# The output projection in two accumulators by halves, 48 weight chunks kept in SBUF, two more kept in PSUM, transposes 32 columns wide

## The chip, the cores and the metric

The kernel runs on one core of a Trainium2 chip. TensorE (PE) multiplies matrices, VectorE (DVE), ScalarE (ACT) and GpSimd (POOL) do the rest, and SyncE (SP) issues most of the DMAs. The metric is the device time of one execution in microseconds; lower is better.

## What is computed

The output is two independent results side by side, each 2048 x 1024 in bf16. A is a long convolution done with FFTs; the change does not touch it. B is a transformer layer over 64 segments of 32 rows, in which 8 memory rows go from one segment to the next:

```python
mem = mem0                                              # 8 x 1024
for s in range(64):
    h = concatenate([mem, x[32*s : 32*s + 32]])         # 40 x 1024
    q, k, v = h @ Wq, h @ Wk, h @ Wv                    # 32 heads of 128: 40 x 4096 each
    p = softmax(where(mask, q @ k.T * 128**-0.5, -1e9)) # per head, 40 x 40
    o = concat_heads(p @ v) @ Wo                        # 40 x 4096 @ 4096 x 1024
    mem, out[s] = o[:8], o[8:]
```

A segment cannot start before the first 8 rows of the one before are done, so the 64 segments run one after the other, and each uses all four weight matrices: 32 MB in bf16, more than SBUF holds.

## The kernel before

**Prologue.** A's stages run first, for some 350 us. Beside and behind them, B's projections of the rows that need no memory are prepared: 24 of the 32 rows go through the segment loop, and the keys, queries and values of the other 8 are computed for all segments at once and stored in DRAM (`REC`, `VBD`). The last of it is the dense value product (`vb_ps`, L765), whose results leave through staging tiles `pair` in the buffers `wring2` and `wring3` by a store into `VBD` on ACT's queue (L768). A planner orders the prologue; the segment loop stands in a block whose order is the program's (`manual_schedule`), so each engine and queue there works in the order of the text, waiting where data or buffers are not ready.

**Chunks.** The weights are cut into 64 chunks of 128 x 2048 (512 KB): 8 for each half (g) of K, Q and V, and 16 for the output (one for two heads). `order` lists them as a segment uses them. 47 are resident in SBUF (`Wmid`, `Wres`, `Wmore`, `Wlate`, `pw`). The other 17, at the places `STREAM` of the order, are copied once to the DRAM buffer `WS` and come from there in each segment through a ring of six slots (`wring`, `RING`): when a chunk's last use is done, `done` gives its slot back and calls `fetch`, which issues the next load in the order on SP's queue (L724). The sixth slot (`wring2`) joins in segment 0 after the chunk at `LATE_SLOT`.

**Kept chunks.** PSUM has columns that the segments do not use. Chunk "A" (an output chunk) is copied there in segment 0 (`keep`), and from segment 1 on it does not come from DRAM: four copies (`quarter`, L817) bring it back to SBUF by quarters, through the buffers `rot` and `QT`, between output chunks. Of chunk "B" five eighths lie in PSUM: the load of the ring brings 768 of its 2048 columns (L721) and `move` (L800) copies the rest from PSUM into the ring slot.

**A segment.** `hT`, the rows of h transposed, comes as the tile `rec` (`load_x`, a POOL DMA, issued when the values' second half is done); the 8 memory columns are put in by `fill_mem`: two transposes of Y on TensorE into `tps` (L862) and a DVE copy into `rec` (L863), in two halves (output columns 0 to 255 and 256 to 511 of both column halves). K half 0 needs chunks 0, 1, 4, 5 from the first fill and 2, 3, 6, 7 from the second, hence `K0_ORDER`. `Proj.run` (L918) takes four products a chunk, each 32 columns of the array wide and 512 columns long, on four column tiles that work side by side. ACT copies an accumulator to `qkv_sb` (L927); four full transposes (L933) and a copy make keys `KT` and queries `QT`. Then scores (L939, L942) into `SB`, softmax on DVE and ACT, attention into `OTp` (L980, L984), ACT's copy to `OT` (L992), and the output: `project` (L1002) takes four products a chunk, 64 columns wide and 512 long, on two column tiles, all into one accumulator `yacc` of one PSUM bank. At the end ACT copies `yacc` to `Y` in two halves (L1078), and the next segment starts with `fill_mem`.

The accumulators `acc` and `yacc` take turns in two PSUM banks (`ps_acc`). Tiles of the pool `one` have one buffer a tag, so a new tile under a tag waits for the last reader of the one before. Two engines' accesses to one PSUM bank of a tile are put in order by waits.

## Time and profile before

| | |
|---|---|
| median of 3 runs | 1903.21 us (1902.97 to 1905.81) |
| the profiled execution | 1907.36 us, span 1905.6 us |
| granted TensorE clock, mean | 0.982 |
| busy: PE, DVE, ACT, POOL | 92%, 45%, 35%, 18% of the span |
| segment 0 starts; its output is stored | 445.8 us; 476.3 us |
| loads of wring: whole; 192 KB | 961; 63 |

PE's busy time is that of matmuls, whose ends are modelled; weight loads run beside them. "Idle before" is the time that an engine stood still ahead of an instruction, with what ended it. A chain of waits is followed back from the last instruction to what released each one. The DMA share is the mean busy share of the core's 16 DMA engines.

### The profile page before, as it was taken

The page shows a single profiled execution, that of the slowest core. Times are in us where ns is not written, and L with a number is a line of the kernel's source. Part 1 is how long each engine was busy: PE and PEld are TensorE (multiplying, and loading weights), DVE is VectorE, ACT ScalarE, POOL GpSimd, SP SyncE. Part 2 cuts the span into 40 slices and gives each one's busy share as a digit, 9 for nine tenths or more (in the row PEclk, how much of TensorE's full clock was granted, in tenths as well). Part 3 has the DMA queues.
Part 4 walks back from the last instruction along what each step waited for, and adds up shares of the span by engine and source line. Part 5 has one row for each costly group of instructions (what it writes and reads, how often), then busy time and mean ns, then how long its engine had stood idle before and what let it go on. Part 6 is the DMA issues. An engine that isn't in the chain of part 4 may idle for free.

```text
span 1905.6 us, 62245 instructions
## 1 busy us (share of the span) xinstructions
PE 1749.0 (92%) x26353; PEld 831.1 (44%) x26353; DVE 853.8 (45%) x2812; ACT 674.8 (35%) x1195; POOL 342.8 (18%) x1014
## 2 busy tenths in 40 slices
PE   6989986778999999999999999999999999999998
PEld 3433322333444444444444444444444444444444
DVE  9927863202344444444444444444443444444443
ACT  6945640112333333333333333333333333333333
POOL 4003341000121111111121111111111111111111
PEclk9999998989999999999999999999999999999999
DMA  9989889998999999999999999999999999999998
GB/s 338 351 302 329 291 271 333 327 284 277 349 373 374 373 378 373 377 372 373 373 373 378 373 376 372 370 372 372 379 374 369 371 378 374 375 373 371 372 379 311
DMA packets 251211, 678.00 MB, mean 356 GB/s; under 512 B 74850, under 2 KB 82930, under 8 KB 250932
## 3 DMA queue, kind: packets, MB, share of 16 engines
q1 hardware_dynamic: 178692, 604.26, 85.0%
q0 software_dynamic: 17488, 46.70, 7.0%
q10 hardware_dynamic: 54752, 23.07, 4.5%
q8 instruction: 206, 3.38, 0.7%
q14 instruction: 73, 0.60, 0.1%
HBM read 618.35 MB, written 59.24 MB: 356 GB/s over the span
## 4 chain that ended last, share of the span: by engine, by line
PE 80%; DMA 7%; DVE 5%; issue 4%; ACT 2%; POOL 0%; ACTq 0%; SPq 0%; DVEq 0%; POOLq 0%
PE acc L918 38%; PE yacc L1002 22%; PE kb_ps L625 5%; PE tps L933 4%; DMA wring<-WS 3%; PE vb_ps L765 3%; DMA REC<-stage 2%; PE OTp L980 1%; ACT s_sb L243 1%; DVE rec L863 1%; PE SB L942 1%; PE tps L862 1%; PE s_ps L241 1%; DMA REC<-xt 1%; PE SB L939 1%
## 5 line engine op out<-in xcount | busy, mean ns | idle before, releaser
L918 PEld LDWEIGHTS <-rec 128*32 128x32 bf16 x12288 | 283.6, 96 | 300.2 <-DVE rec L863 60.7
L927 ACT CAST qkv_sb<-acc 128x512 bf16<-128x512 f32 x384 | 224.7, 585 | 480.0 <-PE acc L918 287.9
L1002 PEld LDWEIGHTS <-OT 128*64 128x64 bf16 x4348 | 255.1, 109 | 195.3 <-ACT OT L992 27.6
L918 PE MATMUL acc<-wring,rec 128*32 128x512 bf16 x2556 | 252.7, 382 | 22.8 <-DVE rec L863 19.1
L918 PE MATMUL acc<-Wres,rec 128*32 128x512 bf16 x3328 | 249.4, 380 | 0.6 <-issue 0.6
L1002 PE MATMUL yacc<-wring,OT 128*64 128x512 bf16 (+1 forms) x1540 | 235.9, 380 | 5.0 <-DMA wring<-WS 4.9
L918 PE MATMUL acc<-Wmid,rec 128*32 128x512 bf16 x3072 | 234.4, 382 | 0.0
L1002 PE MATMUL yacc<-Wmore,OT 128*64 128x512 bf16 (+1 forms) x1280 | 185.4, 381 | 0.0
L817 DVE TENSOR_SCALAR quarter<-OTp 128x256 int32<-128x256 int32 x252 | 101.1, 422 | 187.6 <-ACT OT L992 149.3
L1080 POOL DMA_DIRECT2D out_dram<-Y x128 | 63.7, 502 | 484.5 <-ACT Y L1078 484.2
L918 PE MATMUL acc<-pw,rec 128*32 128x512 bf16 x1796 | 144.8, 382 | 0.1
L1078 ACT CAST Y<-yacc 128x256 bf16<-128x256 f32 x128 | 41.4, 375 | 274.5 <-PE yacc L1002 274.5
L992 ACT CAST OT<-OTp 128x640 bf16<-128x640 f32 x128 | 88.6, 692 | 129.7 <-PE OTp L984 129.0
L918 PE MATMUL acc<-Wlate,rec 128*32 128x512 bf16 x1280 | 104.0, 384 | 17.1 <-DVE rec L863 17.1
L948 DVE TENSOR_REDUCE mx<-SB 128x5 f32<-128x200 f32 x128 | 47.1, 368 | 153.4 <-PE SB L942 153.3
L856 POOL DMA_DIRECT2D rec<-REC x64 | 36.2, 566 | 405.0 <-PE acc L918 372.1
L1002 PE MATMUL yacc<-Wlate,OT 128*64 128x512 bf16 x768 | 105.7, 383 | 0.2 <-ACT OT L992 0.2
L933 PEld LDWEIGHTS <-qkv_sb 128*128 128x128 bf16 x1024 | 57.8, 97 | 109.5 <-ACT qkv_sb L927 108.0
L933 PE MATMUL tps<-ident,qkv_sb 128*128 128x128 bf16 x1024 | 101.6, 222 | 0.4 <-ACT qkv_sb L927 0.3
L893 POOL COPY KT<-rec 128x128 bf16<-128x128 bf16 x128 | 38.2, 298 | 329.4 <-PE SB L942 324.2
L863 DVE COPY rec<-tps 128x32 bf16<-128x32 bf16 x128 | 22.3, 175 | 165.1 <-PE tps L862 115.8
L1027 DVE COPY KT<-tps 128x512 bf16<-128x512 bf16 x64 | 27.1, 424 | 152.2 <-PE tps L933 152.2
(215 smaller groups left out, 2392.9 us busy)
## 6 DMA issues: line engine op xcount, KB each, us to landing
wring<-WS SPq DMA_DIRECT2D x961, 512.0 KB, 6.0
rec<-REC POOLq DMA_DIRECT2D x64, 192.0 KB, 5.8
wring<-WS SPq DMA_DIRECT2D x63, 192.0 KB
SK<-s_sb SPq DMA_DIRECT2D x16, 512.0 KB, 4.8
SU<-s_sb SPq DMA_DIRECT2D x16, 512.0 KB, 4.9
Kg<-SK SPq DMA_DIRECT2D x32, 256.0 KB, 4.2
Ug<-SU SPq DMA_DIRECT2D x32, 256.0 KB, 5.7
REC<-stage ACTq DMA_DIRECT2D x16, 512.0 KB, 10.9
```

The costliest lines, as they stand in the source:

```text
L625: nc.tensor.matmul(ps[:], lhsT=ws[kc][:, hl * 128:(hl + 1) * 128], rhs=xbt(kc).rearrange("p s t -> p (s t)"), start=(kc == 0), stop=(kc == 7))
L765: nc.tensor.matmul(ps[:], lhsT=xbt(kc)[:, 16 * tb:16 * tb + 16, :].rearrange("p s t -> p (s t)"), rhs=ws[kc][:, c * 512:(c + 1) * 512], st ...
L817: nc.vector.tensor_scalar(out=t[:].bitcast(I32), in0=OTi[:, q, 160:416], scalar1=0, scalar2=None, op0=ALU.bitwise_or)
L863: nc.vector.tensor_copy(hT.rearrange("p (dh j) t -> p dh j t", dh=2)[:, :, 2 * half:2 * half + 2, 0:NM], tp.rearrange("p (j dh r) -> p dh ...
L918: nc.tensor.matmul(self.acc[32 * c:32 * c + 32, x - 512 * c:y - 512 * c], lhsT=hT[:, kc, :], rhs=r, start=(n_kc == 0 and x == 512 * c), st ...
L927: nc.scalar.copy(sb[:], self.acc[:])
L933: nc.tensor.transpose(tp[:, i * 128:(i + 1) * 128], sb[:, i * 128:(i + 1) * 128], ident[:])
L948: nc.vector.tensor_reduce(out=mx[:], in_=S, op=ALU.max, axis=AX.X)
L992: nc.scalar.copy(OT[:], o_view)
L1002: nc.tensor.matmul(yacc[64 * dh:64 * dh + m, x - o:y - o], lhsT=lhsT, rhs=r, start=(h == 0 and x == o), stop=(h >= 30), tile_position=(0, ...
L1078: nc.scalar.copy(Y[:, 256 * half:256 * half + 256], yacc[:, 256 * half:256 * half + 256])
L1080: nc.gpsimd.dma_start(bass.AP(outb.tensor, outb.offset + SEG * s * 2048 + 512 * dh, [[2048, 32], [1, 512]]), Y[64 * dh + NM:64 * dh + 40, :])
```

## The change

The output gets two accumulators in two PSUM banks, one for columns 0 to 255 of each half (f = 0), one for 256 to 511. An output chunk is now used in two `out_half` steps of four products, 256 columns long. The first four chunks (`FIRST`) do all of f = 0 before f = 1, and so do the last four (`LAST`). ACT copies the first half to Y between the two halves of `LAST`, and the first `fill_mem` of the next segment stands before the last half chunk. The second fill comes after three chunks of K instead of four.

Every transpose of 128 columns (`turn_tile`) is four products, each of 32 columns on its own column tile.

48 chunks are resident: the new one goes to the buffer `wring2`, which leaves five slots in the ring. 16 chunks are outside, and two of these, A and now all of B (the chunk kc = 4 of K's half 1), stay on chip after segment 0, so 14 are loaded in a segment. B lies in `tps`, `SB`, `OTp` and a small SBUF tile `B_rest`. `quarter_b` copies it by quarters into the buffers of `E` (the exponentials), `QT` and `rot`, and `Proj.add` takes the products in 16 of 128 columns (the last four each in two pieces). The copy of the transposed queries to `QT0` moves from DVE to ACT.

```diff
-STREAM = (0, 5, 10, 15, 21, 26, 31, 36, 41, 46, 49, 52, 54, 57, 60, 61, 63)
-KEPT = {14: "A", 4: "B"}
+STREAM = (1, 7, 13, 18, 20, 24, 30, 35, 41, 46, 49, 53, 56, 59, 60, 62)
+KEPT = {13: "A", 4: "B"}
+FIRST, LAST = (0, 1, 2, 3), (15, 11, 12, 14)
+O_ORDER = (*FIRST, 4, 5, 6, 7, 8, 9, 10, 13, *LAST)
 K0_ORDER = (0, 1, 4, 5, 2, 3, 6, 7)
...
 X_LOAD = 1
-RING = 6
-LATE_SLOT = 4
+RING = 5
...
         order += [(2, kc, g) for kc in range(8)]
-    for hp in range(16):
+    for hp in O_ORDER:
         order.append((3, hp, 0))
...
     loads = [(s, ch) for s in range(n_seg) for ch in order_s
-             if s == 0 and ch not in v_temp[2:] or s > 0 and kept.get(ch) != "A"]
+             if s == 0 and ch not in v_temp[2:] or s > 0 and ch not in kept]
     live = {}
...
             live[s, ch] = k, t = slot()
-            if s > 0 and ch in kept:
-                nc.sync.dma_start(t[:, 0:768], stream_src(ch)[:, 0:768])
-                move(kept[ch], t, True)
-            else:
-                nc.sync.dma_start(t[:], stream_src(ch))
+            nc.sync.dma_start(t[:], stream_src(ch))
...
                     place_late(4, stage_home)
+        place_late(1, lambda: base.tile([128, 2048], BF, tag="wring2", name="Wring"))
         assert len(late) == len(at_hand)
...
     OTi, tpi = OTp[:].bitcast(I32), tps[:].bitcast(I32)
-    homes = {"B": [(OTi[:, :, 416:512], slice(384, 768)), (tpi[:, 1, :], slice(768, 1024))]}
-
-    def move(name, t, back):
-        for p, cols in homes[name]:
-            w = t[:].bitcast(I32)[:, cols]
-            if len(p.shape) == 3:
-                w = w.rearrange("p (b x) -> p b x", b=4)
-            src, dst = (p, w) if back else (w, p)
-            nc.vector.tensor_scalar(out=dst, in0=src, scalar1=0, scalar2=None, op0=ALU.bitwise_or)
+    B_rest = one.tile([128, 4, 32], I32, name="B_rest")
+    B_homes = [tpi[:, 1, :].rearrange("p (c x) -> p c x", c=4),
+               SB[:].bitcast(I32)[:, 200:456].rearrange("p (c x) -> p c x", c=4),
+               OTi[:, :, 416:480], OTi[:, :, 480:512]]
+
+    def bits(dst, src):
+        nc.vector.tensor_scalar(out=dst, in0=src, scalar1=0, scalar2=None, op0=ALU.bitwise_or)
+
+    def quarter_b(q, tag):
+        n = 64 if q < 3 else 32
+        t = one.tile([128, 4, 2 * n], BF, tag=tag, name="quarter_b")
+        bits(t[:].bitcast(I32), B_homes[q])
+        w = [(512 * c + 128 * q, 512 * c + 128 * q + 2 * n, t[:, c, :]) for c in range(4)]
+        if q == 3:
+            w += [(512 * c + 448, 512 * c + 512, B_rest[:].bitcast(BF)[:, c, :]) for c in range(4)]
+        return w
...
             for q in range(4):
-                nc.vector.tensor_scalar(out=OTi[:, q, 160:416].rearrange("p (dh x) -> p dh x", dh=2),
-                                        in0=w[:, q // 2, q % 2], scalar1=0, scalar2=None, op0=ALU.bitwise_or)
+                bits(OTi[:, q, 160:416].rearrange("p (dh x) -> p dh x", dh=2), w[:, q // 2, q % 2])
         else:
-            move(kept[ch], t, False)
+            w = t[:].bitcast(I32).rearrange("p (c f x) -> p f c x", c=4, f=4)
+            for q in range(3):
+                bits(B_homes[q], w[:, q])
+            bits(B_homes[3], w[:, 3, :, 0:32])
+            bits(B_rest[:], w[:, 3, :, 32:64])
...
         t = one.tile([128, 512], BF, tag=("rot", "QT")[q % 2], name="quarter")
-        nc.vector.tensor_scalar(out=t[:].bitcast(I32), in0=OTi[:, q, 160:416], scalar1=0, scalar2=None,
-                                op0=ALU.bitwise_or)
+        bits(t[:].bitcast(I32), OTi[:, q, 160:416])
         return [(o, o + 256, t[:, 256 * dh:256 * dh + 256]) for dh, o in enumerate(quarter_cols(q))]
...
             place_late(1, at_hand[ch][1])
-        elif ch in streamed and (now[0] == 0 or kept.get(ch) != "A"):
+        elif ch in streamed and (now[0] == 0 or ch not in kept):
             if now[0] == 0 and ch in kept:
...
             free.append(live.pop((now[0], ch))[0])
-            i = order_s.index(ch)
-            if now[0] == 0 and i == LATE_SLOT:
-                free.append(2)
-                fetch()
             fetch()
...
+    def turn_tile(dst, src):
+        for e in range(0, 128, 32):
+            nc.tensor.matmul(dst[e:e + 32, :], lhsT=src[:, e:e + 32], rhs=ident[:], start=True, stop=True,
+                             is_transpose=True, tile_position=(0, e))
+
     def fill_mem(hT, Y, half):
...
         for j in (2 * half, 2 * half + 1):
-            nc.tensor.transpose(tp[:, j * 128:(j + 1) * 128], Y[:, j * 128:(j + 1) * 128], ident[:])
+            turn_tile(tp[:, j * 128:(j + 1) * 128], Y[:, j * 128:(j + 1) * 128])
         nc.vector.tensor_copy(
...
     with tc.manual_schedule():
-        for _ in range(RING - 3):
+        for _ in range(RING - 2):
             fetch()
...
+                def add(self, kc, w, start=False, stop=False):
+                    for c in range(4):
+                        for x, y, r in columns(w, 512 * c, 512 * c + 512):
+                            nc.tensor.matmul(self.acc[32 * c:32 * c + 32, x - 512 * c:y - 512 * c],
+                                             lhsT=hT[:, kc, :], rhs=r, start=start and x == 512 * c,
+                                             stop=stop, tile_position=(0, 32 * c))
+
                 def run(self, n=8):
...
                         ch = (self.m, kc, self.g)
-                        w = pieces(ch)
-                        for c in range(4):
-                            for x, y, r in columns(w, 512 * c, 512 * c + 512):
-                                nc.tensor.matmul(self.acc[32 * c:32 * c + 32, x - 512 * c:y - 512 * c],
-                                                 lhsT=hT[:, kc, :], rhs=r, start=(n_kc == 0 and x == 512 * c),
-                                                 stop=(n_kc == 7), tile_position=(0, 32 * c))
-                        done(ch)
+                        if s == 0 or ch not in kept:
+                            self.add(kc, pieces(ch), n_kc == 0, n_kc == 7)
+                            done(ch)
                     self.kc += n
...
                 for i in range(4):
-                    nc.tensor.transpose(tp[:, i * 128:(i + 1) * 128], sb[:, i * 128:(i + 1) * 128], ident[:])
+                    turn_tile(tp[:, i * 128:(i + 1) * 128], sb[:, i * 128:(i + 1) * 128])
                 return tp.rearrange("p (i c r) -> p i c r", i=4, c=4)
...
-            def project(h, w, OT):
+            def project(h, f, w, OT, stop=False):
                 k = 40 * (h % 16)
...
                 for dh in range(2):
-                    o = (h % 2) * 1024 + dh * 512
-                    for x, y, r in columns(w, o, o + 512):
-                        nc.tensor.matmul(yacc[64 * dh:64 * dh + m, x - o:y - o], lhsT=lhsT,
-                                         rhs=r, start=(h == 0 and x == o), stop=(h >= 30),
-                                         tile_position=(0, 64 * dh), skip_group_check=(h == 31))
+                    o = (h % 2) * 1024 + dh * 512 + f * 256
+                    for x, y, r in columns(w, o, o + 256):
+                        nc.tensor.matmul(yacc[f][64 * dh:64 * dh + m, x - o:y - o], lhsT=lhsT,
+                                         rhs=r, start=(h == 0 and x == o), stop=stop,
+                                         tile_position=(0, 64 * dh))
+
+            def out_half(hp, f, OT, stop=False):
+                w = pieces((3, hp, 0))
+                for hh in range(2):
+                    project(2 * hp + hh, f, w, OT, stop and hh == 1)
+                if f == 1:
+                    done((3, hp, 0))
...
                 for hp in hps:
-                    ch = (3, hp, 0)
-                    if s > 0 and kept.get(ch) == "A":
-                        continue
-                    w = pieces(ch)
-                    for hh in range(2):
-                        project(2 * hp + hh, w, OT)
-                    done(ch)
+                    for f in range(2):
+                        out_half(hp, f, OT)
...
                 hp = [ch[1] for ch in kept if kept[ch] == "A"][0]
-                project(2 * hp + q // 2, w, OT1)
-
-            fill_mem(hT, Y, 0)
-            k0 = Proj(0, 0).run(4)
+                project(2 * hp + q // 2, q % 2, w, OT1)
+
+            if s == 0:
+                fill_mem(hT, Y, 0)
+            k0 = Proj(0, 0).run(3)
             fill_mem(hT, Y, 1)
-            k0 = k0.run(4).evac()
+            k0 = k0.run(5).evac()
             q0 = Proj(1, 0).run(4)
...
             q0 = q0.run(4).evac()
-            k1 = Proj(0, 1).run(4)
+            k1 = Proj(0, 1)
+            if s > 0:
+                kb = [ch[1] for ch in kept if kept[ch] == "B"][0]
+                b0, b1 = quarter_b(0, "E"), quarter_b(1, "QT")
+                k1.run(1)
+                k1.add(kb, b0)
+                b2 = quarter_b(2, "E")
+                k1.run(2)
+                k1.add(kb, b1)
+            else:
+                k1.run(4)
             QT0 = one.tile([128, 4, 4, 32], BF, tag="QT", name="QT")
-            nc.vector.tensor_copy(QT0[:], transposes(q0))
-            k1 = k1.run(4).evac()
+            nc.scalar.copy(QT0[:], transposes(q0))
+            if s > 0:
+                b3 = quarter_b(3, "rot")
+                k1.run(3)
+                k1.add(kb, b2)
+                k1.add(kb, b3)
+            k1 = k1.run(8 - k1.kc).evac()
             scores(0, QT0, KT0)
...
             V1 = pv1.evac()
-            yacc = ps_acc.tile([128, 512], F32, tag="acc", name="yacc")
-            out_proj(range(0, 5), OT0)
+            yacc = [ps_acc.tile([128, 512], F32, tag="acc", name="yacc") for f in range(2)]
+            for f in range(2):
+                for hp in FIRST:
+                    out_half(hp, f, OT0)
+            out_proj((4,), OT0)
             attend(1, PT1, V1)
...
             if s == 0:
-                out_proj(range(5, 8), OT0)
-                out_proj(range(8, 16), OT1)
+                out_proj((5, 6, 7), OT0)
+                out_proj((8, 9, 10, 13), OT1)
             else:
                 w0 = quarter(0)
-                out_proj(range(5, 8), OT0)
+                out_proj((5, 6, 7), OT0)
                 w1 = quarter(1)
                 out_quarter(0, w0)
-                out_proj(range(8, 10), OT1)
+                out_proj((8,), OT1)
                 w2 = quarter(2)
                 out_quarter(1, w1)
-                out_proj(range(10, 12), OT1)
+                out_proj((9,), OT1)
                 w3 = quarter(3)
                 out_quarter(2, w2)
-                out_proj(range(12, 14), OT1)
+                out_proj((10,), OT1)
                 out_quarter(3, w3)
-                out_proj(range(14, 16), OT1)
             Y = one.tile([128, 512], BF, tag="PT", name="Y")
-            for half in range(2):
-                nc.scalar.copy(Y[:, 256 * half:256 * half + 256], yacc[:, 256 * half:256 * half + 256])
+            for f in range(2):
+                for hp in LAST:
+                    if f == 1 and hp == LAST[-1] and not last:
+                        fill_mem(pend[s + 1][0], Y, 0)
+                    out_half(hp, f, OT1, hp == LAST[-1])
+                nc.scalar.copy(Y[:, 256 * f:256 * f + 256], yacc[f][:, 0:256])
             for dh in range(2):
```

## The prediction

> **What bounds the kernel now.** I read the page first: the span, the slices, the DMA issues.
>
> ```profile
> span 1905.6 us, 62245 instructions
> ...
> PE   6989986778999999999999999999999999999998
> ...
> DMA  9989889998999999999999999999999999999998
> GB/s 338 351 302 329 291 271 333 327 284 277 349 373 374 373 378 373 377 372 373 373 373 378 373 376 372 370 372 372 379 374 369 371 378 374 375 373 371 372 379 311
> ...
> wring<-WS SPq DMA_DIRECT2D x961, 512.0 KB, 6.0
> rec<-REC POOLq DMA_DIRECT2D x64, 192.0 KB, 5.8
> ...
> wring<-WS SPq DMA_DIRECT2D x63, 192.0 KB
> ```
>
> From slice 11 on (about 480 us) the segments run, and both rows stand at 9: TensorE and the DMA engines are full together. The stage table of one 100 us window says the same more sharply, at the full clock (the column before the last two):
>
> ```profile
> core 0: us, PE busy (x) PEld busy (x) DVE busy (x) ACT busy (x) POOL busy (x), PEclk, DMA share, GB/s
> 1000.00:1100.00 100.00, 95.78 (x1756) 47.32 (x1757) 41.78 (x159) 33.69 (x63) 17.18 (x66) 1.00 1.01 376
> ```
>
> In the list of waits for 1000 to 1210 us, TensorE waits for a streamed chunk for 0.4 us in all. So TensorE's own order sets the pace, with the transfers a hair behind. Next the timeline of one segment's end and the next one's start; the first number is the start.
>
> ```profile
> 1018.78 0.62 PE L1002 MATMUL yacc<-pw,OT 128*64 128x512 bf16 x4
> ...
> 1019.21 0.62 PE L1002 MATMUL yacc<-wring,OT 128*64 128x512 bf16 x4
> ...
> 1019.87 0.65 ACT L1078 CAST Y<-yacc 128x256 bf16<-128x256 f32 x2 [4.20 <-PE yacc L1002]
> ...
> 1020.30 0.28 PE L862 MATMUL tps<-ident,Y 128*128 128x128 bf16 x2 [0.46 <-ACT Y L1078]
> 1020.68 0.17 DVE L863 COPY rec<-tps 128x32 bf16<-128x32 bf16 x1 [0.89 <-issue]
> ...
> 1020.91 0.40 PE L918 MATMUL acc<-wring,rec 128*32 128x512 bf16 x4 [0.32 <-DVE rec L863]
> 1021.13 0.82 PE L918 MATMUL acc<-Wlate,rec 128*32 128x512 bf16 x12
> ...
> 1021.88 0.28 PE L862 MATMUL tps<-ident,Y 128*128 128x128 bf16 x2
> ...
> 1022.44 0.40 PE L918 MATMUL acc<-Wlate,rec 128*32 128x512 bf16 x4 [0.27 <-DVE rec L863]
> ...
> 1023.96 0.39 PE L918 MATMUL acc<-Wmid,rec 128*32 128x512 bf16 x4
> ...
> 1024.28 0.40 PE L933 MATMUL tps<-ident,qkv_sb 128*128 128x128 bf16 x4
> ...
> 1024.61 0.61 PE L918 MATMUL acc<-Wmid,rec 128*32 128x512 bf16 x8
> ...
> 1027.65 0.19 PE L939 MATMUL SB<-KT,QT 128*32 128x40 bf16 x4
> ...
> 1027.90 0.63 PE L918 MATMUL acc<-pw,rec 128*32 128x512 bf16 x8
> ```
>
> Starts give the rates, since matmul ends are modelled. A projection chunk (four products) takes 0.217 us, an output chunk 0.43 us. The chain of waits puts the next segment's first product here, so a segment is 1043.42 - 1020.91 = 22.51 us; over segments 5 to 59 the mean issue-to-issue step of the output stores is 22.59 us.
>
> ```profile
> 1043.42 1.05 PE acc L918 x16
> ```
>
> **The change, part by part**, per segment, as TensorE time.
>
> *The end of a segment.* Before: the last output chunk streams until 1019.21 + 0.43 = 19.64, the next projection starts at 20.91: 1.27 us for two copies of Y, two transposes and a copy into rec. The half banks let ACT copy columns 0 to 255 (0.375 us) while TensorE does three half chunks (0.65 us) of the other bank; the copy and its signals need 0.6 us (yacc end to transposes: 19.64 to 20.30, less the 0.1 us that any change to transposes costs), so they are covered. What stays is the transposes (0.11 us as below), two changes of product shape at about 0.1 us each (a projection to an output product starts 0.31 us after it where 0.217 is the rule), and the way transposes, DVE, projection: transposes stream until 1022.04, restart 1022.44, so 0.40 us, of which the last half chunk and its shape change hide 0.32. Total 0.39; saved 0.88 us.
>
> *The second half of Y* is turned after three chunks instead of four. Before, from 1021.78 (end of the twelve) to 1022.44: 0.66 us. Now one chunk (0.217) stands inside the 0.40 us, and the transposes take 0.11: 0.29 left; saved 0.37 us. The three chunks (0.65 us) cover the second copy of Y (0.6 us) barely; uncovered it costs 0.1.
>
> *32-wide transposes.* Four products of 32 columns each replace one. From 1023.96 + 0.217 = 24.18 to 24.61 one set of four transposes costs 0.43 us today. No row shows a 32-wide transpose. Nearest below: the 32 score products, same contraction and width on the four column tiles, in 0.25 us (27.65 to 27.90), 7.8 ns each; a 128-column stream on four tiles is a quarter of a 512-column one, 0.217/16 = 13.6 ns. I take 13.8 ns, 0.22 us a set, since streams of this length are what the projection row measures. Upper end: no overlap between tiles, 0.217/4 = 54 ns each, 0.87 us a set. The shape change falls away, but the ACT copy before a set (ends 0.06 us after TensorE is ready for K0 and for Q1) then shows, and for Q0 it shows by 0.15, as the two quarters of B are shorter than the chunk they displace. Savings 0.15 + 0.06 + 0.21 + 0.15 = 0.57 us.
>
> A page of the Trainium skill speaks against this step (TensorE: Matmul & The Clock Gate, "Wait — 56ns, not 53.3ns?"): starts of matmuls never come closer than about 25 ns, however short. By that rule the 80 small transposes would cost 0.9 us more and the time would be an estimated 1863 us; this trace's score products start 7.8 ns apart, so I go by the row.
>
> *Halves of output chunks.* 128 products of 256 columns for 60 of 512 and 8 of 256. Two quarter products take 0.11 us (1017.15 to 1017.26), half a 512 pair is 0.1075: 64 pairs x 0.0025 = +0.16 at most, I take +0.10. With one chunk instead of two between quarters of A, quarter 1 (DVE copy 0.42 us, may start 0.17 us after the last use of OT0) comes late behind 0.11 + 0.43 us: +0.09.
>
> *Kept chunk B.* 20 short products for 4: +0.02. DVE copies three 256-word quarters at 0.42 us and two of 128 words, estimated 0.29 from a 0.155 us base, for 0.56 + 0.41 today; it waits on TensorE for E and rot only. Their cover is q0's second half and k1 (each copy has at least 0.4 us before its use), but the last starts after Q0's transposes, with two chunks and a quarter (0.49 us) to be done in: +0.04. QT0 moves from DVE (0.425) to ACT (0.587 us); k1's copy stands behind it on ACT, and k1 ends 0.9 us later, so nothing. Without these covers the copies would add up to 1.8 us. SP loses the wait on DVE that the partial reload caused.
>
> Sum: 0.88 + 0.37 + 0.57 - 0.10 - 0.09 - 0.02 - 0.04 = 1.57; TensorE needs 20.94 us.
>
> *Transfers.* Before, a segment moves 15 x 0.524 + 0.197 MB of weights, 0.197 of rec and 0.131 of V rows and output: 8.39 MB in 22.51 us is 373 GB/s, which is the row above. Now 14 x 0.524 + 0.328 = 7.67 MB: 20.6 us at that rate, 20.7 with a third more PE code (instruction fetches are 3 x 16 KB a segment, 0.2 us of the engines' time). So it falls in step with TensorE and again ends just below it. The Trainium skill names about 358 GB/s as a core's share of HBM (DMA: Bandwidth & Descriptors, "Where 436 GB/s comes from"); that would make 21.4 us, an estimated 1828 us in all, but the window shows 376.
>
> *Ring.* Six slots become five. From a release to the use five chunks on, my chunk order gives 5.4 to 7.4 us, 6.7 on average (before: about 8), against 6.0 us median landing, which shrinks if fewer are queued. I allow 0.11 us a segment of waits: lower end 0, upper end 0.8 (two windows under 6.1 us).
>
> *rec* is needed 0.9 us earlier relative to its issue. It landed 0.3 to 2.6 us before its use, five times under 0.9: 0.02 us, in the allowance.
>
> *Once:* the 48th resident chunk (k0, fifth in use) goes into wring2, where the last VBD store must land first; behind it on SP wait three ring loads. Today the sixth slot waits there:
>
> ```profile
> SPq L724 <- DMA VBD<-pair: 6.5, 1, 6.5
> ```
>
> Segment 0 took 30.5 us (445.8 to 476.3), 8 above the others. The new wait is a store of 4 to 8 us plus a 4.5 us load, less 1.5 us: 7 to 11. I take 0 for the difference, -3 to +8.
>
> Result: 22.59 - (20.94 + 0.11) = 1.54 us x 63 = 97 us. The profiled execution took 1907.36 us around its span of 1905.6; it would take 1810. The median of the runs is 4.15 us lower: 1903.21 - 97 = 1806.
>
> **Rivals.**
> *Ring bound.* Five slots leave TensorE waiting for wring chunks by 0.5 to 0.9 us. For: DMA share of 1.01 and 6.0 us landings. Against: 0.4 us of such waits in 210 us with six. T = 21.7: 1903 - 0.85 x 63 = 1849 us.
> *Transfers give more.* If the DMA engines can exceed 376 GB/s and the covers leave less than I counted, T = 20.5, 1771 us. Against: full share, landings of four chunk times.
> *Slower: the transposes do not overlap.* 80 small ones a segment at 54 ns instead of 13.8 are +3.2 us: T = 24.3, 1903 + 107 = 2010 us. It decides from 13.8 + 1540/80 = 33 ns each. For: full transposes now start 83 ns apart, far above 54. Against: the score products overlap on the same tiles.
>
> **How the numbers follow.** Forecast (1785 to 1832) 0.60, ring bound or small transposes between 20 and 30 ns (to 1885) 0.20, more than forecast 0.07, transposes serial or another wait of over 1.5 us a segment 0.13. The range 1770 to 1862 reaches the first three but for the tail of the second. A measurement of this kernel tells 0.2% (4 us) from nothing: faster 0.85, same 0.02, slower 0.13.
>
> **What would show it.** Right: a step of 20.9 to 21.2 us; transposes in 0.2 to 0.25 us a set; the 0.89 us idle before DVE rec gone; 14 wring loads a segment; DMA share near 1.00. Wrong: transposes starting over 30 ns apart; TensorE waiting for wring by over 0.3 us a segment; DVE quarter_b on the chain; a segment 0 beyond 38 us.

## The result and the profile after

The changed kernel takes 1984.0 us in the median of 4 runs (1976.02 to 1999.71) against 1903.09 (1902.07 to 1905.81) for the kernel before: a ratio of 1.0433, 95% interval 1.036 to 1.0506. The forecast of 1806 us, faster, was wrong in size and in sign. The profiled execution of the changed kernel is the slowest of its four runs, 1999.71 us, so its segment figures lie about 0.25 us above the median run's (16 us over 63 segments).

From the page of the changed kernel (span, the slices of DMA share and of GB/s, queues, chain by engine, loads of the ring):

```profile
span 1997.9 us, 79472 instructions
...
DMA  9989879988999999998999989999898898899997
GB/s 322 357 309 341 291 231 350 307 240 290 325 319 331 326 327 330 329 332 305 337 332 324 325 317 328 323 318 331 323 322 318 308 328 311 317 321 322 327 325 260
...
q8 instruction: 274, 4.49, 0.9%
...
PE 66%; DMA 21%; issue 7%; DVE 2%; ACT 2%; ACTq 1%; POOL 0%; SPq 0%; another core or an unknown queue 0%; POOLq 0%; DVEq 0%
...
wring<-WS SPq DMA_DIRECT2D x897, 512.0 KB, 5.9
```

The same two parts of the page before, which the prediction did not show:

```profile
q8 instruction: 206, 3.38, 0.7%
...
PE 80%; DMA 7%; DVE 5%; issue 4%; ACT 2%; POOL 0%; ACTq 0%; SPq 0%; DVEq 0%; POOLq 0%
```

The loads are fewer, as meant (897 against 961 whole ones and 63 partial ones), but the row of GB/s no longer stands at 373 in the segments: it stands near 322, and the DMA row has 8s in it. So the transfers are not the bound, although the DMA engines' share of the chain of waits has grown from 7 to 21% (theory R below takes this up). The same window as before says it more sharply; the clock in it is full, and both TensorE (95.78 before) and the DMA engines (1.01 before) have idle time:

```profile
1000.00:1100.00 100.00, 90.51 (x2172) 60.27 (x2168) 39.91 (x152) 32.99 (x61) 15.61 (x56) 1.00 0.92 326
```

The step from one output store to the next is 23.94 us on average (22.63 by the same count before, 22.59 over segments 5 to 59); the forecast was 21.05. The timeline shows which parts came as forecast and which did not. First column the start; in brackets the idle time before the first of the group and what ended it:

```profile
1017.60 1.04 PE L922 MATMUL acc<-Wres,rec 128*32 128x512 bf16 x16
1018.47 0.20 PE L950 MATMUL SB<-KT,QT 128*32 128x40 bf16 x3
1019.81 0.18 PE L950 MATMUL SB<-KT,QT 128*32 128x40 bf16 x1 [1.14 <-issue]
1019.81 0.20 PE L953 MATMUL SB<-KT,QBm 128*32 128x40 bf16 x4
...
1029.34 0.41 PE L1013 MATMUL yacc<-wring,OT 128*64 128x256 bf16 x4
1029.68 0.29 PE L864 MATMUL tps<-ident,Y 128*32 128x128 bf16 x8
1029.91 0.41 PE L1013 MATMUL yacc<-pw,OT 128*64 128x256 bf16 x4
1030.31 0.40 PE L922 MATMUL acc<-Wlate,rec 128*32 128x512 bf16 x4
...
1030.97 0.28 PE L864 MATMUL tps<-ident,Y 128*32 128x128 bf16 x8
1031.08 0.39 PE L922 MATMUL acc<-Wlate,rec 128*32 128x512 bf16 x4
1031.54 0.40 PE L922 MATMUL acc<-Wring,rec 128*32 128x512 bf16 x4
...
1033.32 0.41 PE L864 MATMUL tps<-ident,qkv_sb 128*32 128x128 bf16 x16
1033.55 0.39 PE L922 MATMUL acc<-Wmid,rec 128*32 128x512 bf16 x4
```

The lower part is the change at work: 16 narrow transposes take 0.23 us (33.32 to 33.55), and the first fill hides behind half chunks. The upper part is new. In the middle of 32 score products, of which 3 are done and whose operands are all there, TensorE stands for 1.14 us and waits for nothing that the profile shows ("issue"). The list of TensorE's waits from 500 to 1880 us says that this is the rule (total us, times, longest):

```profile
PE acc L922 <- issue: 50.4, 35, 3.0
PE tps L864 <- issue: 22.4, 13, 2.7
PE acc L922 <- DMA wring<-WS: 14.8, 32, 2.1
PE SB L950 <- issue: 14.0, 9, 2.3
PE SB L953 <- issue: 11.0, 8, 1.9
```

In the same list of the kernel before, the line for waits of `acc` for issue is

```profile
PE acc L918 <- issue: 0.6, 1, 0.6
```

Counting every stretch of over 0.35 us between the starts of two following TensorE instructions (matmuls and weight loads) that has no releaser, "gaps" from here on, I get 2.44 us a segment after and 0.02 before (0.10 with the stretch right behind the first store, where the granted clock is 0.5 from 472.5 to 482.7 us). A gap is counted from start to start, so it holds a little work too: the list of waits, which counts idle time alone, has 1.9 us a segment for issue.

About 2.2 of the 2.44 us have one cause, below. The other 0.2 us are 34 products, each over 0.35 us behind the weight load before it, in stretches where the granted clock is 0.5: from 923.2 to 926.6 us, for one. The trace's clock rows have seven such stretches of 3.4 us between the first and the last output store, 11.9 us of full clock lost; the kernel before has the one of 10.2 us, 5.1 us lost. So at most 7 us of the difference are the clock's.

What the longer gaps have in common is their place in the instruction stream. 79 of them are longer than 0.5 us, and all 79 lie at the same position (161) when TensorE's instructions are numbered from the start and the number is taken modulo 256. Queue 8 of the page, kind "instruction", brings packets of 16,384 bytes; by 256 instructions that is 64 bytes each. Each of the 79 gaps ends 1.2 to 1.6 us after the end of such a packet (median 1.43). So TensorE has used up one piece of its program and waits for the next. There are 274 pieces where the kernel before had 206.

One further cost is paid once. The first output is stored at 486.4 us instead of 476.3, and among TensorE's waits of 440 to 500 us is the 48th resident chunk:

```profile
PE acc L922 <- DMA Wring<-in_B_Wk_dram: 11.8, 1, 11.8
```

### The profile page after: what moved, and what is told of

It reads as the page before. It is cut to its first block, busy times and chain, and to the rows that moved or that the text cites. A ratio compares the mean times of both kernels' runs of the same rounds, so it can differ in the third digit from the quotient of the medians.

```text
span 1997.9 us, 79472 instructions
## 1 busy us (share of the span) xinstructions
PE 1754.1 (88%) x35013; PEld 1050.9 (53%) x35045; DVE 858.6 (43%) x2877; ACT 716.6 (36%) x1259; POOL 344.8 (17%) x1013
## 4 chain that ended last, share of the span: by engine, by line
PE 66%; DMA 21%; issue 7%; DVE 2%; ACT 2%; ACTq 1%; POOL 0%; SPq 0%; another core or an unknown queue 0%; POOLq 0%; DVEq 0%
PE acc L922 28%; PE yacc L1013 21%; DMA wring<-WS 15%; PE kb_ps L626 4%; PE tps L864 3%; DMA REC<-stage 3%; PE vb_ps L762 2%; PE OTp L991 1%; ACT s_sb L244 1%; PE SB L953 1%; DMA VBD<-pair 1%; PE SB L950 1%; DMA KS_nat<-in_A_ssm_k_dram 1%; PE s_ps L242 1%; ACTq L655 1%
## 5 line engine op out<-in xcount | busy, mean ns | idle before, releaser
L922 PEld LDWEIGHTS <-rec 128*32 128x32 bf16 x13296 | 325.0, 97 | 360.7 <-issue 129.2
L1013 PEld LDWEIGHTS <-OT 128*64 128x64 bf16 (+1 forms) x8192 | 434.0, 109 | 61.4 <-ACT OT L1003 26.1
L922 PE MATMUL acc<-Wres,rec 128*32 128x512 bf16 x3328 | 264.2, 387 | 24.0 <-issue 24.0
L1013 PE MATMUL yacc<-wring,OT 128*64 128x256 bf16 (+1 forms) x2568 | 236.5, 274 | 4.4 <-DMA wring<-WS 2.2
L1013 PE MATMUL yacc<-Wmore,OT 128*64 128x256 bf16 (+1 forms) x3072 | 233.7, 273 | 0.1
L864 PE MATMUL tps<-ident,qkv_sb 128*32 128x128 bf16 x4096 | 111.5, 223 | 24.4 <-issue 24.2
L864 PEld LDWEIGHTS <-qkv_sb 128*32 128x32 bf16 x4096 | 74.6, 97 | 95.3 <-ACT qkv_sb L938 49.3
L1013 PE MATMUL yacc<-Wlate,OT 128*64 128x256 bf16 x1536 | 120.3, 276 | 4.5 <-issue 4.3
L922 PE MATMUL acc<-Wlate,rec 128*32 128x512 bf16 x1280 | 121.7, 382 | 0.8 <-issue 0.8
L626 PE MATMUL kb_ps<-XBT,pw 128*128 128x512 bf16 x313 | 85.4, 398 | 9.9 <-ACT stage L615 7.8
```

What stands on the lines that cost most here:

```text
L626: nc.tensor.matmul(ps[:], lhsT=ws[kc][:, hl * 128:(hl + 1) * 128], rhs=xbt(kc).rearrange("p s t -> p (s t)"), start=(kc == 0), stop=(kc == 7))
L864: nc.tensor.matmul(dst[e:e + 32, :], lhsT=src[:, e:e + 32], rhs=ident[:], start=True, stop=True, is_transpose=True, tile_position=(0, e))
L922: nc.tensor.matmul(self.acc[32 * c:32 * c + 32, x - 512 * c:y - 512 * c], lhsT=hT[:, kc, :], rhs=r, start=start and x == 512 * c, stop=sto ...
L1013: nc.tensor.matmul(yacc[f][64 * dh:64 * dh + m, x - o:y - o], lhsT=lhsT, rhs=r, start=(h == 0 and x == o), stop=stop, tile_position=(0, 64 ...
```

## The theories

**F (fetch).** The narrow transposes and half products raise TensorE's instructions in a segment and make them short. Where 256 instructions pass in about 4 us, the next piece, whose transfer lies among the weight loads, comes too late.

**R (ring).** Five slots instead of six are too few: the loads start later, TensorE waits for chunks, and the DMA engines run at a share of 0.91 to 0.92.

**T (transposes).** The narrow transposes are dearer than 14 ns, in the records or behind them.

## Experiments

Figures by segment are means between the first and the last output store of one profiled execution each, the gaps and the waits for ring chunks counted from start to start. "Pieces" is the count of queue 8's packets.

| kernel | median us | ratio to before, 95% | step us | pieces | gaps us | waits for ring chunks us |
|---|---|---|---|---|---|---|
| before | 1903 to 1905 | | 22.63 | 206 | 0.02 | 0.02 |
| after | 1984.0 | 1.036 to 1.0506 | 23.94 | 274 | 2.44 | 0.57 |
| full_turn | 1932.5 | 1.0112 to 1.0177 | 22.91 | 244 | 0.80 | 0.34 |
| half_loads | 1832.6 | 0.9597 to 0.9644 | 21.30 | 274 | 0.08 | 0 |
| before_turn32 | 1955.3 | 1.0233 to 1.0284 | 23.42 | 236 | 1.57 | 0.03 |
| before_ring5 | 2009.9 | 1.0536 to 1.06 | 24.20 | 206 | 0.57 | 1.02 |
| after_ring6 | 1984.7 | 1.0365 to 1.0455 | 23.87 | 274 | 2.60 | under 0.01 |
| before_split | 1912.4 | 1.0025 to 1.0053 | 22.66 | 236 | 0.03 | 0.01 |
| lean5 | 1919.3 | 1.005 to 1.0092 | 22.75 | 222 | 0.60 | 0.44 |
| lean6 | 1890.3 | 0.9901 to 0.9943 | 22.29 | 222 | 0.43 | 0.02 |

### full_turn: the changed kernel with full transposes

```diff
     def turn_tile(dst, src):
-        for e in range(0, 128, 32):
-            nc.tensor.matmul(dst[e:e + 32, :], lhsT=src[:, e:e + 32], rhs=ident[:], start=True, stop=True,
-                             is_transpose=True, tile_position=(0, e))
+        nc.tensor.transpose(dst, src, ident[:])
```

> The changed kernel with full 128-wide transposes again: 20 products a segment where it has 80, so TensorE runs 920 instructions (weight loads and products) in a segment for 1040. Theory F: TensorE runs out of instructions; the 79 stalls of the changed kernel that no wait explains (2.18 us a segment) come from its program arriving in 16 KB pieces of 256 instructions behind the weight loads, and a piece lasts too short now. Then these stalls fall below 1.2 us a segment, while TensorE's own work grows by 0.57 us: step 22.3 to 23.2 us, 1880 to 1940 us. Rival R: the ring of five slots costs the time; then nothing is won and the transposes' 0.57 us come on top: step 24.3 to 24.6, 2005 to 2030 us. Rival T: the 32-wide transposes themselves are slow; then all of the loss goes: under 1860 us.

Measured: 1932.52 us (1925.0 to 1939.04), 51 us less than the changed kernel, although each set of transposes is longer again. TensorE's waits from 500 to 1880 us:

```profile
PE acc L920 <- issue: 14.1, 21, 1.3
PE yacc L1011 <- issue: 9.4, 11, 1.2
PE acc L920 <- DMA wring<-WS: 7.1, 20, 1.2
```

The wait of `acc` for issue falls from 50.4 to 14.1 us; the gaps fall by 1.64 us a segment, and the step by 1.03. This is inside what F had expected, and outside R's and T's ranges. The narrow transposes cost the changed kernel more than they save, and what they cost is gaps. A third of the gaps stays, so the rest of the change makes some too.

### half_loads: the same program, half the bytes

From segment 1 on, a load brings half the columns of its chunk, and the products of the other half read the same columns again; the output of these chunks' second halves is therefore not the reference's. TensorE's instructions are those of the changed kernel.

```diff
-            nc.sync.dma_start(t[:], stream_src(ch))
+            n = 2048 if s == 0 else 1024
+            nc.sync.dma_start(t[:, 0:n], stream_src(ch)[:, 0:n])
...
-        return [(0, 2048, live[now[0], ch][1][:])]
+        t = live[now[0], ch][1]
+        if now[0] > 0:
+            return [(0, 1024, t[:, 0:1024]), (1024, 2048, t[:, 0:1024])]
+        return [(0, 2048, t[:])]
```

> The changed kernel in which, from segment 1 on, each ring load brings only the first 1024 of a chunk's 2048 columns and the products read these twice, so the output is not the reference's: the same instructions, half the weight traffic. F, with the program's pieces waiting behind the weight loads: the unexplained stalls fall below 0.4 us a segment and the waits for wring vanish, step 20.9 to 21.4 us, 1790 to 1825 us. F, with the pieces slow by themselves: wring waits vanish (0.56 us), the stalls stay above 1.5 us: step 22.6 to 23.4, 1900 to 1950 us. R: the waits for wring go and the rest stays, the same 1900 to 1950 us, with stalls not tied to the pieces.

Measured: 1832.6 us (1827.94 to 1836.56), a median step of 21.20 us. The window of 1000 to 1100 us, and the line of its waits from 500 to 1880 us for `acc` products that wait for issue:

```profile
1000.00:1100.00 100.00, 99.23 (x2474) 64.74 (x2461) 46.66 (x182) 39.05 (x72) 17.02 (x62) 1.00 0.61 191
```

```profile
PE acc L926 <- issue: 0.3, 1, 0.3
```

With the same 274 pieces the gaps are gone (0.08 us a segment), and TensorE is at 99%. So the number of instructions alone does not starve it; the data beside the pieces do. The trace has the mechanism: half of the pieces start within 1.19 us of TensorE's passing the boundary of 256, where it was 2.54 us in the changed kernel; the transfer itself takes 1.0 us in both. This run also gives TensorE's own work in the changed kernel, 21.20 us where I had summed 20.94. The step is within F's expectation; the time is a little above it since segment 0 still has the 12.0 us wait for the 48th chunk.

### before_turn32: the kernel before with narrow transposes alone

```diff
+    def turn_tile(dst, src):
+        for e in range(0, 128, 32):
+            nc.tensor.matmul(dst[e:e + 32, :], lhsT=src[:, e:e + 32], rhs=ident[:], start=True, stop=True,
+                             is_transpose=True, tile_position=(0, e))
...
-            nc.tensor.transpose(tp[:, j * 128:(j + 1) * 128], Y[:, j * 128:(j + 1) * 128], ident[:])
+            turn_tile(tp[:, j * 128:(j + 1) * 128], Y[:, j * 128:(j + 1) * 128])
...
-                    nc.tensor.transpose(tp[:, i * 128:(i + 1) * 128], sb[:, i * 128:(i + 1) * 128], ident[:])
+                    turn_tile(tp[:, i * 128:(i + 1) * 128], sb[:, i * 128:(i + 1) * 128])
```

> The kernel before with 32-wide transposes alone: 910 instructions a segment for 790, the ring and the transfers as before. TensorE's own work falls by about 0.6 us to 21.9, the transfers stay at 22.4 to 22.5. F: unexplained stalls appear, 0.3 to 1.2 us a segment, all at one place modulo 256 of TensorE's instruction stream; step 22.5 to 23.2 us, 1900 to 1945 us. R: no such stalls, the transfers set the step: 22.4 to 22.6, 1890 to 1905 us. T: each set of four takes longer than the 0.43 us of before: above 1920 us with stalls inside the transposes.

Measured: 1955.33 us (1947.93 to 1956.96), above my expectation: I had put the gaps at no more than 1.2 us a segment, and they are 1.57. TensorE's waits, 500 to 1880 us:

```profile
PE acc L923 <- issue: 28.1, 32, 1.7
...
PE tps L861 <- issue: 11.8, 13, 1.9
```

The shortest step is 21.82 us, 0.68 below the shortest before, so where no gap falls the transposes save about what I said they would. The time lies in T's range too, but a set of 16 takes 0.23 us here, 0.43 before, and the gaps stand where F had them: nearly all of the time is at position 161 again, whatever the product. The one edit thus makes the gaps by itself, in the old order, with six slots and all loads.

### before_ring5: the kernel before with five slots

```diff
             free.append(live.pop((now[0], ch))[0])
-            i = order_s.index(ch)
-            if now[0] == 0 and i == LATE_SLOT:
-                free.append(2)
-                fetch()
             fetch()
```

> The kernel before with five ring slots: wring2 stays unused after the prologue. Nothing else changes, 790 instructions a segment. R: TensorE waits for wring by 0.8 us a segment or more: 1950 us and above. F: the ring costs what the changed kernel's waits for wring are, 0.3 to 0.6 us a segment: 1915 to 1945 us, and no stall without a cause. If the ring costs nothing, below 1910 us.

Measured: 2009.87 us (2006.77 to 2019.05), above what F and inside what R had expected. A slot less costs this kernel 1.57 us a segment. TensorE's waits, 500 to 1880 us:

```profile
PE tps L858 <- DVE wring L800: 55.8, 57, 1.0
...
PE yacc L998 <- DMA wring<-WS: 27.5, 44, 1.5
```

Part of it is chunk B: DVE's copy of five eighths of it into its ring slot (L800) now comes late, and the transposes of Y at the start of a segment (L858) wait for it. Part of it is the clock: between the output stores the granted clock is 0.5 for 44 us in all, 22 us of full clock lost against 5 before, about 0.27 us a segment. The 0.57 us of gaps in the table are of this kind, products 0.4 us behind what stands before them; only one of 83 lies at a boundary of 256. So R is a real cost in the old order, and far more than the 0.11 us that I allowed. Whether it costs the changed kernel anything, where B is no longer copied into the ring, needed a run of its own.

### after_ring6: the changed kernel with six slots again

The 48th resident chunk gives `wring2` back to the ring; its products read another resident chunk in its place, so the keys of half 0 are not the reference's. Loads and instructions stay those of the changed kernel.

```diff
-RING = 5
+RING = 6
+LATE_SLOT = 5
...
-        place_late(1, lambda: base.tile([128, 2048], BF, tag="wring2", name="Wring"))
+        res[late.pop(0)] = res[0, 3, 0]
...
             free.append(live.pop((now[0], ch))[0])
+            if now[0] == 0 and order_s.index(ch) == LATE_SLOT:
+                free.append(2)
+                fetch()
             fetch()
...
```

> The changed kernel with the sixth ring slot back: the 48th resident chunk has no buffer and its products read another resident chunk, so the output is not the reference's; instructions and the 14 loads a segment are the changed kernel's. F (the program's pieces come late): the waits for wring (0.56 us) fall below 0.15, the unexplained stalls stay at 2.0 us a segment or more, since deeper queues do not bring the pieces sooner: step 23.1 to 23.9 us, 1925 to 1980 us. R (the ring sets it): step 21.2 to 21.7 us, 1810 to 1840 us, the stalls largely gone. Both, each hiding part of the other: between.

Measured: 1984.65 us (1970.56 to 1990.15), no different from the changed kernel: a little above F's range for the time, its step of 23.87 us within it, and far above R's range. TensorE's waits, 500 to 1880 us:

```profile
PE acc L926 <- issue: 61.4, 40, 2.7
PE tps L868 <- issue: 27.9, 15, 2.8
PE SB L954 <- issue: 13.2, 10, 2.6
```

Waits for ring chunks fall to nothing, and the gaps grow from 2.44 to 2.60 us. From 500 to 1880 us the DMA share is 0.92 and the rate 324 GB/s, against 0.91 and 323 with five slots. With no wait left for a chunk, the loads hold TensorE up only through the pieces that they delay, and its stalls keep the next loads waiting for a slot. R does not explain the changed kernel. The run also shows the once-only cost: without the 48th chunk's load the first output is stored at 472.1 us, not 486.4. These 14 us do not show in the median, so the segments of the median run are not faster, if anything 0.2 us slower, which is no more than the spread of the runs.

### before_split: the kernel before with its output products halved

```diff
-                    for x, y, r in columns(w, o, o + 512):
-                        nc.tensor.matmul(yacc[64 * dh:64 * dh + m, x - o:y - o], lhsT=lhsT,
-                                         rhs=r, start=(h == 0 and x == o), stop=(h >= 30),
-                                         tile_position=(0, 64 * dh), skip_group_check=(h == 31))
+                    for f in (0, 256):
+                        for x, y, r in columns(w, o + f, o + f + 256):
+                            nc.tensor.matmul(yacc[64 * dh:64 * dh + m, x - o:y - o], lhsT=lhsT,
+                                             rhs=r, start=(h == 0 and x == o), stop=(h == 31 or h == 30 and f == 256),
+                                             tile_position=(0, 64 * dh), skip_group_check=(h == 31))
```

> The kernel before with each output product of 512 columns cut into two of 256: 120 more instructions a segment, as many as the narrow transposes bring, but all where they are far apart (256 instructions last 7 us there). If the spacing decides, 256 instructions against the time a piece takes, then stalls under 0.4 us a segment and 1903 to 1930 us. If the number of instructions a segment decides: as the narrow transposes alone, 1940 to 1960 us.

Measured: 1912.41 us (1907.71 to 1914.55), 0.4% slower. Its page and that of before_turn32 have the same line of queue 8:

```profile
q8 instruction: 236, 3.87, 0.8%
```

and yet, in its waits from 500 to 1880 us, TensorE waits for issue of an `acc` product once, not 32 times:

```profile
PE acc L918 <- issue: 0.3, 1, 0.3
```

The same number of pieces, 0.03 against 1.57 us of gaps. The added instructions lie here among the output products, where a half product starts 54 ns after the one before (0.217 us for four), so that 256 instructions, 128 products and their weight loads, are 6.9 us of work; 128 narrow transposes are 1.8 us (0.23 us for 16). Measured in the traces, with the gap itself taken out of the time of a run of 256:

| | 256 instructions take under 5 us | a piece is there after the boundary, median (5 to 95%) | gaps over 0.5 us |
|---|---|---|---|
| after | 46% of the runs | 4.98 us (3.65 to 6.70) | 79 |
| before_turn32 | 47% | 5.25 us (3.98 to 6.26) | 79 |
| before_split | 10% | 4.99 us (3.99 to 6.61) | 3 |
| half_loads | 49% | 3.73 us (2.83 to 4.87) | 3 |
| full_turn | 11% | 5.16 us (3.91 to 6.49) | 47 |

"There" is the end of the packet plus the 1.43 us after which the gaps end. Both sides matter: dense runs with late pieces starve (the first two rows); long runs with late pieces, or dense runs with early pieces, do not. The last row does not fit a mark of 5 us: full_turn has few runs under it and still 47 gaps, 0.5 to 1.6 us long. It fits when each run is held against its own piece. Behind full_turn's gaps of over 0.5 us stand runs that take 5.14 us (median) and pieces that are there after 6.17; its other runs take 6.34 us with pieces there after 4.95. In the changed kernel the four numbers are 4.21 and 6.08, 6.11 and 4.42. And in the nine kernels other than before, at 2023 boundaries, the first instruction behind a boundary never starts less than 1.19 us after the end of its piece's packet. Why the late pieces are late one by one I have not found out.

### lean5 and lean6: the halves only where they pay

Both keep the early first half of Y and the chunks A and B on chip, and take back the narrow transposes and most of the half products: output chunks run whole into one accumulator, and only the second half (f = 1) of `LAST` goes to a second bank, whose sum DVE adds. lean5 has the changed kernel's 48 chunks and five slots:

```diff
...
-            yacc = [ps_acc.tile([128, 512], F32, tag="acc", name="yacc") for f in range(2)]
-            for f in range(2):
-                for hp in FIRST:
-                    out_half(hp, f, OT0)
-            out_proj((4,), OT0)
+            yacc = ps_acc.tile([128, 512], F32, tag="acc", name="yacc")
+            out_proj((0, 1, 2, 3, 4), OT0)
...
+            for hp in LAST:
+                out_half(hp, 0, OT1)
+            nc.scalar.copy(Y[:, 0:256], yacc[:, 0:256])
+            rest_y = one.tile([128, 256], F32, tag="E", name="rest_y")
+            nc.scalar.copy(rest_y[:], yacc[:, 256:512])
+            part = ps_acc.tile([128, 512], F32, tag="acc", name="part")
+            for hp in LAST:
+                if hp == LAST[-1] and not last:
+                    fill_mem(pend[s + 1][0], Y, 0)
+                out_half(hp, 1, OT1, part)
+            nc.vector.tensor_tensor(out=Y[:, 256:512], in0=part[:, 256:512], in1=rest_y[:], op=ALU.add)
...
```

> The changed kernel with few instructions: full transposes, output products 512 columns long except in the last four chunks, whose second halves go to a second bank and are added on DVE. 830 instructions a segment; ring of five, 14 loads, the overlapped end of a segment stays. F: unexplained stalls under 0.5 us, wring waits 0.3 to 0.6 us on TensorE's own 21.6: step 22.1 to 22.7 us, 1875 to 1920 us. R: the ring of five costs as in the kernel before, 1.5 us: 23.1 and more, above 1940 us.

lean6 has 47 resident chunks, six slots, and so 15 loads a segment:

```diff
-STREAM = (1, 7, 13, 18, 20, 24, 30, 35, 41, 46, 49, 53, 56, 59, 60, 62)
-KEPT = {13: "A", 4: "B"}
+STREAM = (1, 7, 13, 18, 20, 24, 30, 35, 41, 46, 49, 51, 53, 56, 59, 60, 62)
+KEPT = {14: "A", 4: "B"}
...
-RING = 5
+RING = 6
+LATE_SLOT = 5
...
```

> As the lean kernel with six slots and 47 resident chunks; A and B stay on chip, so 15 loads a segment: 8.19 MB, 22.0 us at 373 GB/s. F: the transfers and TensorE's 21.6 us meet, stalls under 0.4 us, few wring waits: step 22.0 to 22.5 us, 1865 to 1898 us, and faster than the kernel before. If the loads cannot go past what the kernel before shows, 1890 to 1910 us.

Measured: lean5 1919.29 us (1915.14 to 1922.34), lean6 1890.3 (1885.1 to 1892.54). lean5 is 0.7% slower than before: its time and its waits for the ring are inside F's ranges, its gaps (0.60 us, under 0.5 expected) and its step (22.75, up to 22.7 expected) just outside. lean6 is faster than both kernels, by 0.8% of before: ratio 0.9922, interval 0.9901 to 0.9943. Its time and step are in the first range that was expected, its gaps of 0.43 us a little over 0.4. Its window of 1000 to 1100 us, and its waits from 500 to 1880 us:

```profile
1000.00:1100.00 100.00, 98.34 (x1846) 51.14 (x1840) 45.02 (x173) 35.86 (x67) 16.02 (x57) 1.00 0.99 367
```

```profile
PE acc L923 <- issue: 7.6, 17, 0.7
...
PE yacc L1017 <- DMA wring<-WS: 0.9, 2, 0.5
```

TensorE is at 98% and the DMA engines at 0.99 again. Between lean5 and lean6 the ring's waits fall from 0.44 to 0.02 us a segment, at the price of one load more; the step falls by 0.46. So here, unlike in the changed kernel, the sixth slot seems to pay. It is not tested alone: lean6 also has one resident chunk less and other places of the streamed chunks.

## Why the prediction was wrong

**The step that failed** is the term for TensorE's program. I did count it: "with a third more PE code (instruction fetches are 3 x 16 KB a segment, 0.2 us of the engines' time)". The count was right (206 to 274 pieces, a third more), but I priced it as load on the DMA engines alone. I did not ask whether TensorE has to wait for a piece, how long a piece takes to come behind 512 KB loads, and how fast 256 of the new instructions go by. The price was some 2.2 of the 2.44 us of gaps a segment in the profiled run, more than the whole saving of 1.57. No rival had it either: the one that ended on the slower side had the narrow transposes serial at 54 ns, and the 0.23 us a set refute that. Only the words "or another wait of over 1.5 us a segment", inside the chance of 0.13, cover what happened, and they name no cause.

A page of the Trainium skill has the fetch itself (Runtime: NRT & Kernel Launch, "Instruction fetch mechanics"): instructions come in blocks of 16 KiB, 256 each, and the cost of crossing a block is "mostly hidden". The trace agrees on the block: packets of 16,384 bytes and gaps 256 apart. It differs on the cost: with the DMA engines at a share of 0.9, 79 crossings cost 0.5 to 3.4 us each.

The other terms, per segment, against the timeline above and that of half_loads, which has next to no gaps:

- **End of a segment** (saved 0.88 forecast): from 1029.34, less two half chunks of 0.217 us, to 1030.31 are 0.54 us that are not products, 1.27 before. Saved 0.73: I had left too little for the way from the half chunk through DVE to the projection.
- **Second half of Y** (0.37): 1030.31 to 1031.54 holds four projection chunks and 0.36 us more, 0.66 before. Saved 0.30.
- **32-wide transposes** (0.57): K0, Q0, K1 and Q1 with the waits ahead of them take 0.27, 0.40, 0.23 and 0.28 us in the two timelines, against 0.43 each: saved 0.54. At 0.23 us for 16 they start 14.4 ns apart, 13.8 forecast. By the floor of about 25 ns that the Trainium skill states (TensorE: Matmul & The Clock Gate, "Wait — 56ns, not 53.3ns?"), which I had weighed and set aside, it would have been an estimated 0.40 us. The measurement decides for the row of the score products.
- **Halved output products** (+0.10): before_split has them alone and all of them, at +0.03 us in the step.
- **Quarters of A** (+0.09): no wait of TensorE for a quarter stands in the changed kernel's list from 500 to 1880 us.
- **Chunk B** (+0.06 in two terms): the stretch with its last quarters takes 0.70 us (median in half_loads), 0.15 us longer than its products.
- **Sum**: 1.39 instead of 1.57 us, TensorE's own work 21.20 instead of 20.94. As a step that would be well within the range. The forecast's sum also had a slip: it took 20.94 from the 22.51 us of one segment and subtracted it from the mean of 22.59, which counts 0.08 us a segment, 5 us in all, as saved. From median to median the step falls by 1.32 us, 22.52 to 21.20.
- **Transfers** (20.6 to 20.7 us at 373 GB/s): not tested at that load. No run has 14 whole loads and no gaps. lean6 moves 15 at 367 GB/s in the window above, 370 from 500 to 1880 us, with a share of 0.99, so the rate holds where TensorE lets it.
- **Ring** (0.11, at most 0.8): 0.57 us in the changed kernel counted from start to start, 0.26 as idle time in the list above, both inside the bounds; but after_ring6 shows that these waits are not added to the gaps, they take their place. As a rival, "ring bound" had about the right cost for a kernel with few gaps (lean5, 0.44 us) and was far too small for the old order (1.57 us).
- **Once** (0, -3 to +8): +10 us. The wait itself, 11.8 us, was in the estimate of 7 to 11 us and a little over; I had set it off in full against segment 0's old delay of 8 us, but before, the waits of TensorE for ring chunks in segment 0 sum to 4.6 us only.

Of the signs that I named, "a step of 20.9 to 21.2" and "DMA share near 1.00" failed, "0.2 to 0.25 us a set" and "14 wring loads" came true. "The 0.89 us idle before DVE rec gone" was no good sign: that is idle time of DVE, which stands 2.49 us idle before its first copy into `rec` now; what shrank is TensorE's time between products, 1.27 to 0.54 us. Of the signs of being wrong, two came true: waits for wring of over 0.3 us a segment, by the count from start to start, and a segment 0 beyond 38 us (447.6 to 486.4). Neither points at the cause. Adding up: 63 x (21.30 - 22.63), the mean steps of half_loads and before, is -84 us, gaps +149 (2.44 less the 0.08 that half_loads has), ring +36, segment 0 +10: +111, where the profiled executions differ by 92. The 19 us that are too much are 0.3 us a segment, which fits a gap's length being counted from start to start, product included, and a gap that covers other waits; I did not separate these.

**What stays open.** The traces show that a piece starts later when more data are on the way (2.54 against 1.19 us), not by what rule the DMA engines choose between it and the loads, nor when TensorE asks for it. Why the granted clock falls to 0.5 in short stretches is open too: between the first and the last output store the changed kernel, after_ring6 and before_ring5 have 7 to 12 of them, the other kernels at most one.

## What to carry to other kernels

Count instructions as a resource with a rate: where the DMA engines are full, take a stretch of 256 TensorE instructions (weight loads count) and see that it lasts as long as a piece of the program takes to come, here 4 to 7 us. Cutting wide operations into narrow ones can save array time (here 0.43 us to 0.23 for a set of transposes) and spends that rate, so cut only where the stretch around is slow, or where the cut itself is worth it. A gap in the bounding engine with no releaser, at a fixed distance in instructions, is the mark to look for.

## What the hardware did that I had not expected

- TensorE can run dry of instructions in straight-line code: 79 gaps of over 0.5 us, up to 3.35 us, each at a multiple of 256 instructions from the others and each ended 1.2 to 1.6 us after a 16,384-byte packet on queue 8.
- The gaps followed the data load, not only the code: halving the bytes of the loads removed them (2.44 to 0.08 us a segment) with the same 274 pieces.
- The same 30 pieces more cost 1.57 us a segment as transposes among dense work and 0.03 us as halves of long products.
- Products of 32 columns on four column tiles start 14.4 ns apart for a 128-column stream.
- A ring slot was worth 1.57 us a segment in the kernel before, some 0.27 us of it by a lower granted clock, and nothing measurable in the changed kernel.
